# Reordering the first block of a Fourier mixing and squared-ReLU kernel: front before weight rounding, and one rounding moved into the transform

## The chip, the cores and the metric

One core of a Trainium2 chip runs the whole program. The metric is device microseconds (us) of one execution. Faster or slower means a difference of at least 2%. Engines: PE (TensorE matmul), PEld (its weight load), DVE (VectorE), ACT (ScalarE), POOL (GpSimd), SP (SyncE, which issues the loads).

## The reference, cut to what matters

```python
# x: (8, 3008, 256) float32; w_in: (256, 2048) and w_out: (2048, 256), both float64
X = np.fft.fft(np.fft.fft(x, axis=1), axis=2).real.astype(np.float32)
t = X.reshape(8 * 3008, 256)
h = t @ w_in
g = np.maximum(h, 0) ** 2
return (g @ w_out).astype(np.float32)
```

## The kernel before

The kernel folds x and makes, for each batch, three small spectra P, E and Q by products with cosine and sine tables (`dft_ops`). The transform over the 256 features is folded into w_in: for each of 8 pairs of 128-column slices of w_in, PE makes G1 and G2 ("G products", PSUM tile `pg`) and one column gE (`pe`). After that the program is a row of steps, one for each block of columns and pair j. A step has three parts:

- **front**: four products on PE into two PSUM tiles (`ph`), then `he` and two `g` for each half on DVE;
- **combine**: relu and square on ACT, then four additions on POOL (the "left sums" s1 to s4);
- **back**, two steps later: seven products on PE into four accumulators.

The weights come as float64 and are rounded to float32 on the chip (`convert`): for a pair of w_in ("win") or of w_out ("wout") a start (two DVE operations, L201 and L206, and three on ACT, L203, L204 and L208) and a finish (three DVE operations, L211, L213 and L214). A wout also needs four subtractions on POOL (the "weight sums"). Only the first block's eight steps do this; in all later steps the weights stay.

The parts that the change and the argument touch (cuts are marked):

```python
psh = ctx.enter_context(tc.tile_pool(name="psh", bufs=2, space=PSUM))   # ph and pg share it
psd = ctx.enter_context(tc.tile_pool(name="psd", bufs=2, space=PSUM))   # pd, pe, po

def load_win(j):
    w = ep.tile([P, 2, CH], F32, name="win", tag="sB" if j % 2 else "sA")
    finish = convert(w, pair_in(j))          # start now, finish later
    def then():
        finish()
        for tab, G, n in ((cosd, G1, P), (sind, G2, P - 1)):
            ps = psh.tile([P, CH], F32, name="pg", tag="h")
            ...                              # products; ACT copies to G
        ps = psd.tile([P, CH], F32, name="pe", tag="d")
        ...                                  # products; ACT copies to gE
    return then

weights = [lambda j=j: load_win(j) for j in range(2)]
for j in range(NJ):                          # NJ = 8
    if j + 2 < NJ:
        weights.append(lambda j=j: load_win(j + 2))
    weights.append(lambda j=j: load_wout(j))

def next_weight():                           # start the next, finish the one begun
    nonlocal begun
    then, begun = begun, weights.pop(0)() if weights else None
    then()
...
    # one turn of the loop over the steps
    if i < NJ:
        for _ in range(2 if i + 2 < NJ else 1):
            next_weight()                    # roundings and G products of pair i + 2
    g = front(b, k0, n, j, between)
    ...
    if i >= LAG and flight:                  # LAG = 2
        back(at[2], at[3], g_, s_, final)
    ...
    flight.append(((b, k0, n, j), g, combine(n, g)))
```

## Time and profile before

| What | Value |
|---|---|
| Time, median of 3 runs | 2051.64 us |
| Time, median of 6 runs (with the later ones) | 2051.55 us (2050.50 to 2052.09) |
| PE busy | 2004.4 of 2049.8 us |
| PE's first row, front 0 on DVE, front 8 on DVE | 11.9, 70.42, 134.35 us |
| One step of a later block on PE | 4.67 us |

The reader should take from the profile that PE does all it can from 160 us on, so the change plays entirely in the first 135 us, where DVE's roundings hold PE up. In a timeline row the bracket gives the time that the engine stood idle just before the row and what released it. The lines themselves stand in the prediction below.

### The profile page before, as it was taken

To read this page: it belongs to the slowest core of one execution; us is meant where nothing else is said; L and a number is where in the kernel's file an instruction comes from. 1 tells how busy PE (TensorE), PEld (TensorE's weight loads), DVE (VectorE), ACT (ScalarE), POOL (GpSimd) and SP (SyncE) were. 2 spreads that over 40 slices of the span, in tenths; PEclk is the share of its full clock that TensorE was granted. 3 is DMA by queue.
4 is the path that set the end of the run, shared out by engine and by line. 5 is a ranking of instruction groups with operands and counts; after the bars stand their busy time and mean duration, and the time that the engine had idled before them with its cause. 6 is when DMAs were issued, how large, how long until landed. Compare 5 with 4: busy or idle time off the path is not lost.

```text
span 2049.8 us, 27083 instructions
## 1 busy us (share of the span) xinstructions
PE 2004.4 (98%) x9464; PEld 1743.8 (85%) x9464; DVE 1337.7 (65%) x3275; ACT 952.2 (46%) x1067; POOL 1203.9 (59%) x1763
## 2 busy tenths in 40 slices
PE   6799999999999999999999999999999999999998
PEld 4588888888888888888888888888888888888887
DVE  6798666776567755777557775677656776555554
ACT  1564444544444444445444544454444444445443
POOL 0376555665556655666557665666655675556654
PEclk9899999999999999999999999999999999999999
DMA  6223000110011000011001110011001100000000
GB/s 178 88 57 59 29 11 32 41 36 21 11 41 41 26 26 30 26 31 46 11 26 36 38 29 11 31 41 36 21 11 41 41 11 16 31 11 11 21 11 20
DMA packets 66104, 68.45 MB, mean 33 GB/s; under 512 B 26297, under 2 KB 56969, under 8 KB 65968
## 3 DMA queue, kind: packets, MB, share of 16 engines
q1 hardware_dynamic: 64892, 66.21, 11.3%
q8 instruction: 74, 1.21, 0.3%
q10 hardware_dynamic: 1076, 0.52, 0.1%
q14 instruction: 62, 0.51, 0.1%
HBM read 42.03 MB, written 24.68 MB: 33 GB/s over the span
## 4 chain that ended last, share of the span: by engine, by line
PE 95%; DVE 3%; DMA 1%; issue 0%; SPq 0%; ACT 0%; DVEq 0%
PE ph L405 16%; PE mA L448 16%; PE ph L406 16%; PE mC L448 16%; PE mB L448 16%; PE mD L448 8%; PE pd L345 5%; PE po L490 2%; PE pg L229 1%; DMA xt<-in_x_dram 1%; DVE he L408 0%; DVE g L411 0%; PE pe L235 0%; DVE g L410 0%; DMA raw<-in_moe_w_in_dram 0%
## 5 line engine op out<-in xcount | busy, mean ns | idle before, releaser
L419 ACT ACTIVATE g<-g 128x1004 f32<-128x1004 f32 (+1 forms) x384 | 399.4, 1040 | 739.3 <-DVE g L411 481.9
L408 DVE SCALAR_TENSOR_TENSOR he<-Et,gE,ph 128x251 f32<-128x251 f32 (+1 forms) x768 | 362.1, 472 | 578.2 <-PE ph L406 577.7
L425 POOL TENSOR_TENSOR s<-g 128x251 f32<-128x251 f32 (+1 forms) x384 | 252.2, 657 | 671.2 <-ACT g L420 650.6
L405 PE MATMUL ph<-Pt,G 128*128 128x251 f32 (+1 forms) x1536 | 452.4, 375 | 0.5 <-DVE g L411 0.4
L406 PE MATMUL ph<-Qt,G 127*128 127x251 f32 (+1 forms) x1536 | 451.2, 374 | 0.0
L420 ACT ACTIVATE g<-g 128x1004 f32<-128x1004 f32 (+1 forms) x384 | 399.3, 1040 | 12.1
L448 PE MATMUL mA<-g,wout 128*128 128x251 f32 (+1 forms) x1536 | 389.6, 375 | 0.0
L448 PE MATMUL mC<-s,wsum 128*128 128x251 f32 (+1 forms) x1536 | 389.5, 374 | 0.0
L410 DVE TENSOR_TENSOR g<-he,ph 128x251 f32<-128x251 f32 (+1 forms) x768 | 320.6, 417 | 58.9 <-DVE he L408 0.5
L405 PEld LDWEIGHTS ph<-Pt,G 128*128 128x128 f32 x1536 | 287.8, 189 | 42.0 <-issue 3.2
L406 PEld LDWEIGHTS ph<-Qt,G 127*128 127x128 f32 x1536 | 291.2, 190 | 35.8
L448 PEld LDWEIGHTS mC<-s,wsum 128*128 128x128 f32 x1536 | 291.6, 190 | 35.3
L411 DVE TENSOR_TENSOR g<-he,ph 128x251 f32<-128x251 f32 (+1 forms) x768 | 314.2, 409 | 0.0
L448 PEld LDWEIGHTS mA<-g,wout 128*128 128x128 f32 x1536 | 281.5, 189 | 37.3 <-issue 4.0
L426 POOL TENSOR_TENSOR s<-s,g 128x251 f32<-128x251 f32 (+1 forms) x384 | 289.3, 753 | 30.1
L427 POOL TENSOR_TENSOR s<-g 128x251 f32<-128x251 f32 (+1 forms) x384 | 290.7, 757 | 0.0
L428 POOL TENSOR_TENSOR s<-g,s 128x251 f32<-128x251 f32 (+1 forms) x384 | 263.6, 686 | 0.0
L448 PE MATMUL mB<-g,wsum 128*128 128x251 f32 (+1 forms) x768 | 225.1, 374 | 0.0
L448 PE MATMUL mD<-s,wout 128*128 128x251 f32 (+1 forms) x768 | 225.0, 374 | 0.0
L448 PE MATMUL mB<-s,wout 128*128 128x251 f32 (+1 forms) x768 | 224.6, 374 | 0.0
L448 PEld LDWEIGHTS mB<-g,wsum 128*128 128x128 f32 x768 | 145.7, 190 | 17.7
L448 PEld LDWEIGHTS mD<-s,wout 128*128 128x128 f32 x768 | 144.9, 189 | 18.1
(77 smaller groups left out, 1334.1 us busy)
## 6 DMA issues: line engine op xcount, KB each, us to landing
xt<-in_x_dram SPq DMA_DIRECT2D x24, 512.0 KB
out_dram<-os SPq DMA_DIRECT2D x94, 125.0 KB
out_dram<-os SPq DMA_DIRECT2D x80, 126.0 KB
xt<-in_x_dram SPq DMA_DIRECT2D x16, 384.0 KB
Et<-e_dram SPq DMA_DIRECT2D x7, 752.5 KB
raw<-in_moe_w_in_dram SPq DMA_DIRECT2D x16, 256.0 KB
raw<-in_moe_w_out_dram SPq DMA_DIRECT2D x16, 256.0 KB
xt<-in_x_dram SPq DMA_DIRECT2D x8, 480.0 KB
```

Of the source, the lines that this page charges most:

```text
L405: nc.tensor.matmul(hP, G1[:, fs], pt[:, ks], start=True, stop=True)
L406: nc.tensor.matmul(hQ, G2[:, fs], qt[:, ks], start=True, stop=True)
L408: nc.vector.scalar_tensor_tensor(out=t, in0=et[:, ks], scalar=gE[:, fc:fc + 1], in1=hP, op0=ALU.mult, op1=ALU.add)
L410: tt(out=g[:, h, 0, 0:n], in0=t, in1=hQ, op=ALU.add)
L411: tt(out=g[:, h, 1, 0:n][:, ::-1], in0=t, in1=hQ, op=ALU.subtract)
L419: act(v, v, AF.Relu)
L420: act(v, v, AF.Square)
L425: gt(out=s1, in0=g21, in1=g22, op=ALU.add)
L426: gt(out=s2, in0=s1, in1=g11, op=ALU.subtract)
L427: gt(out=s3, in0=g11, in1=g21, op=ALU.subtract)
L428: gt(out=s4, in0=g12, in1=s2, op=ALU.subtract)
L448: nc.tensor.matmul(acc[nm][:, i, 0:n], w, v[:, 0:n], start=j == 0 and i == 0, stop=j == NJ - 1, skip_group_check=True)
```

## The change: its intent, and the diff

The intent is to start the steps earlier and to take the roundings out of the way of each step's products. In the prologue, the rounding of pair 1 moves into the gaps that DVE has while PE makes Q, and Q's joins come after both of its odd products. In a step, the front comes first, then relu, square and left sums, then the G products of the *next* pair (rounded a step ago), then the roundings: wout of this pair, win two pairs ahead.

```diff
-        return then
+        return finish, products          # load_win: G products are a part of their own
@@ weights
     for j in range(NJ):
+        weights.append(lambda j=j: load_wout(j))
         if j + 2 < NJ:
             weights.append(lambda j=j: load_win(j + 2))
-        weights.append(lambda j=j: load_wout(j))
@@ groups of the transform: odd products and their join are two entries now
-            return [(0.5, even_n), (0.5, join_4), (0.7, join_2), (1.2, odd_n)]
+            return [(0.5, even_n), (0.5, join_4), (0.7, join_2), (0.0, odd_n), (1.2, join_1)]
@@ prologue (the P and E groups are reordered in the same way; cut)
+    groups_at(20, 25)                    # Q: both even groups
     begun = weights.pop(0)()             # start of win 1
-    groups_at(16, 20, 17, 18, 19, 21, 22, 23)
-    next_weight()
+    groups_at(21, 22, 23)                # Q: joins and odd products of the first
+    products = next_weight()             # finish of win 1
+    groups_at(26, 27, 28, 24, 29)        # second's joins and odd products, then both last joins
+    products = [products]
@@ the step
-            if i < NJ:
-                for _ in range(2 if i + 2 < NJ else 1):
-                    next_weight()
             g = front(b, k0, n, j, between)
+            if i < NJ:
+                s = combine(n, g)
+            for f in products:
+                f()
+            products = [next_weight() for _ in range(2 if i + 2 < NJ else 1 if i < NJ else 0)]
```

More of the change, by code (lines that the diff above doesn't have):

```diff
@@ L222, in load_win, with products @@
         finish = convert(w, pair_in(j))
-        def then():
-            finish()
+        def products():
             for tab, G, n in ((cosd, G1, P), (sind, G2, P - 1)):
@@ L253, in then @@
             gt(out=t4, in0=t2, in1=b21, op=ALU.subtract)
-        return then
+        return then, lambda: None
     folded = {}
@@ L374, in odd_n, with join_1 @@
             def odd_n():
-                ps = psd.tile([P, 512], F32, name="pd", tag="d")[0:n, 0:n0]
-                product(ps, 3)
+                st["odd"] = psd.tile([P, 512], F32, name="pd", tag="d")[0:n, 0:n0]
+                product(st["odd"], 3)
+            def join_1():
                 dst = e_rows if b is None else PQE[b][which]
                 nh = S // 8
-                both(dst[:, kp:kp + 2 * n0 - 1:2], dst[:, M - kp - 2 * (nh - 1):M - kp + 1:2], st["c"], ps)
-            return [(0.5, even_n), (0.5, join_4), (0.7, join_2), (1.2, odd_n)]
+                both(dst[:, kp:kp + 2 * n0 - 1:2], dst[:, M - kp - 2 * (nh - 1):M - kp + 1:2], st["c"],
+                     st["odd"])
+            return [(0.5, even_n), (0.5, join_4), (0.7, join_2), (0.0, odd_n), (1.2, join_1)]
         ops = [] if b is None else [(0.0, start)]
@@ L504 @@
     for j in range(NJ):
+        weights.append(lambda j=j: load_wout(j))
         if j + 2 < NJ:
             weights.append(lambda j=j: load_win(j + 2))
-        weights.append(lambda j=j: load_wout(j))
     def next_weight():
         nonlocal begun
-        then, begun = begun, weights.pop(0)() if weights else None
-        then()
+        (finish, products), begun = begun, weights.pop(0)() if weights else None
+        finish()
+        return products
     pieces = [[f for _, f in fold(0, t)] for t in range(NT)]
@@ L536 @@
     for_p(0)
-    begun()
+    finish, products = begun
+    finish()
+    products()
     for t in range(1, 4):
         for_p(t)
-    groups_at(0, 4)
+    groups_at(0, 5)
     for_p(4)
@@ L543 @@
     for_p(5)
-    groups_at(5, 6)
+    groups_at(6, 7)
     for_p(6)
+    groups_at(3)
     for n, t in enumerate((4, 5, 6, 0, 1, 2, 3)):
         for_q(t)
-        groups_at(*((3, 7), (8,), (9, 10), (11, 12), (13, 14), (15,), ())[n])
+        groups_at(*((4, 8, 9), (10,), (11, 12), (13, 14, 15), (16, 17), (18,), (19,))[n])
+    groups_at(20, 25)
     begun = weights.pop(0)()
-    groups_at(16, 20, 17, 18, 19, 21, 22, 23)
-    next_weight()
+    groups_at(21, 22, 23)
+    products = next_weight()
+    groups_at(26, 27, 28, 24, 29)
+    products = [products]
     LAG = 2
@@ L595 @@
         if i < len(steps):
-            flight.append(((b, k0, n, j), g, combine(n, g)))
+            flight.append(((b, k0, n, j), g, s if i < NJ else combine(n, g)))
 _INS = ['x', 'moe_w_in', 'moe_w_out', 'cos_s', 'sin_s', 'cos_d', 'sin_d', 'alt_d']
```

## The prediction

> **What bounds the kernel now.** I read the page's busy shares and slices first, then the windows view over stretches that I chose from the slices, then the timelines of PE, DVE, ACT and POOL from 36 to 135 us.
>
> From the page and from the windows view (columns: stretch, its length, busy us of PE, PEld, DVE, ACT, POOL with instruction counts, granted PE clock, DMA share, GB/s):
>
> ```profile
> PE 2004.4 (98%) x9464; PEld 1743.8 (85%) x9464; DVE 1337.7 (65%) x3275; ACT 952.2 (46%) x1067; POOL 1203.9 (59%) x1763
> ...
> PE   6799999999999999999999999999999999999998
> ...
> DVE  6798666776567755777557775677656776555554
> ...
> PEclk9899999999999999999999999999999999999999
> ...
> 11.91:69.30 57.39, 45.77 (x133) 30.42 (x133) 40.88 (x111) 9.66 (x23) 0.86 (x2) 0.82 0.47 129
> 69.30:119.20 49.90, 36.85 (x165) 30.80 (x164) 44.96 (x79) 33.79 (x55) 25.42 (x39) 0.90 0.30 94
> 119.20:160.00 40.80, 40.42 (x195) 35.66 (x195) 35.88 (x80) 22.87 (x27) 30.45 (x46) 1.00 0.41 63
> 160.00:2030.00 1870.00, 1869.92 (x8925) 1637.10 (x8924) 1206.21 (x2983) 878.93 (x954) 1140.53 (x1664) 1.00 0.09 27
> ```
>
> PE is the bound: from 160 to 2030 us it is busy 1869.92 of 1870. Nothing in the change shortens that stretch, whose code stays as it is. All that it can win lies between 11.9 us, where PE starts, and 119.2 us, after which PE hardly waits. There PE stands idle 11.6 us up to 69.3 us (transform, first weights) and 13.1 us from there to 119.2 us (steps 0 to 5 of the first block), and its clock is granted at 0.82 and 0.90, so some products take double time. Even all of the idle time, 24.7 us, is 1.2% of 2051.6.
>
> What holds PE there is the loop of DVE and PE (columns: start, length, engine, line, op, out<-in, count, idle before and its releaser):
>
> ```profile
> 65.50 0.72 ACT L204 ACTIVATE fd<-fd,ramp 128x512 uint32<-128x512 f32 x1
> ...
> 66.25 0.69 DVE L211 SCALAR_TENSOR_TENSOR fd<-raw,fd 128x512 uint32<-128x512 uint32 x1 [3.42 <-ACT fd L204]
> ...
> 70.42 0.47 DVE L408 SCALAR_TENSOR_TENSOR he<-Et,gE,ph 128x251 f32<-128x251 f32 x1 [2.15 <-PE ph L406]
> ...
> 73.42 0.68 DVE L211 SCALAR_TENSOR_TENSOR fd<-raw,fd 128x512 uint32<-128x512 uint32 x1
> ...
> 76.99 1.20 DVE L211 SCALAR_TENSOR_TENSOR fd<-raw,fd 128x512 uint32<-128x512 uint32 x1
> ...
> 80.94 0.48 DVE L408 SCALAR_TENSOR_TENSOR he<-Et,gE,ph 128x251 f32<-128x251 f32 x1 [0.99 <-PE ph L406]
> ...
> 75.49 1.86 PE L229 MATMUL pg<-win,cosd 128*128 128x256 f32 x4 [4.26 <-DVE win L214]
> ...
> 116.56 1.13 PE L229 MATMUL pg<-win,cosd 128*128 128x256 f32 x4 [1.35 <-DVE win L214]
> ...
> 76.00 0.79 POOL L426 TENSOR_TENSOR s<-s,g 128x251 f32<-128x251 f32 x1
> ```
>
> The reader is to see three things. PE waits at each step for the rounding of the next pair (win L214), 4.26 us at worst. DVE waits little inside steps (0.99 us), so it is nearly the bound of these steps: 44.96 us busy of 49.9. And the first step's DVE work starts at 70.42 only, though Q, its last input, was ready at 56.7 us: DVE idles 3.42 and 2.15 us there, because ACT's share of the rounding (L203, L204) queues behind ACT copies that wait for PE.
>
> **What the Trainium skill says.**
> - "TensorE: Matmul & The Clock Gate", section "What's actually happening": after an idle window of about 3.4 us PE's clock is halved, and it takes a busy window to get it back. The trace agrees: the pg products (first of eight to last) take 3.57 us after the gap of 4.26 us and 1.99 us after one of 1.35 us.
> - The same page, "Architectural detail": ACT, DVE and GpSimd queues are strict FIFO. So program order decides; the wait of 3.42 us is of this kind.
> - "SBUF — State Buffer", "Who interferes with whom": a DVE instruction with two SBUF inputs contends with a GpSimd instruction that reads SBUF; one with at most one does not. The trace agrees: L211 takes 0.68 us with POOL idle and 1.20 at 76.99 beside POOL's left sums (the row at 76.00 is one of them); the front's DVE work (one input in PSUM) keeps its 0.42 and 0.47 us beside POOL's weight sums at 80 to 82 us.
> - "Perfetto Trace Analysis", "GPSIMD Engine Instruction": POOL spans are to be timed from start to start. I do so.
>
> **The change part by part.** Costs, all from the DVE, ACT and PE timelines, start to start. A front on DVE (he, g, g twice): 70.42 to 72.75 = 2.33 us. A rounding (L201, L206, L211, L213, L214): 72.75 to 75.43 = 2.68 us alone; beside the left sums 75.47 to 79.88 = 4.41, so 1.73 us more. Relu and square on ACT: POOL starts 2.3 us after the front. PE at full clock: front 1.70, back 2.97, one pair's G products 2.65 (116.56 to 119.20).
>
> (a) Removed from ahead of the first front: products of pairs 1 and 2 on PE (59.37 to 69.4) and the roundings of win 2 and wout 0. Pair 1's rounding moves into DVE's gaps while PE makes Q: those are 1.88, 3.82 and 1.28 us now (idle times in DVE's timeline, 45 to 56 us). ACT's copies for Q now go ahead of that pair's ACT work. I work Q out anew: last odd E join to 44.9; Q's second even group on PE to 48; ACT done with L204 at 48.2; win 1 rounded at 50.3; second joins to 51.3; the odd products, back to back, to 54 or (slow clock) 55.3; join 1 of the second to 55 or 56.3; first ph to +0.5. So the first front starts on DVE at about 56.2 instead of 70.42: 14.2 us earlier.
>
> (b) Given back: before, 14 roundings (win 1 to 7, wout 0 to 6) lie ahead of front 6 and front 6 starts at 125.95. After, wout 6 moves behind it: one rounding less, but the two of step 0 now stand between front 0 and front 1. So between front 0 and front 6 lie 12 roundings after, 10 before: 2 x 2.68 us plus contention come back.
>
> (c) Period of a step after: DVE front 2.33, two roundings 5.36, together 7.69. The left sums run on POOL from 4.6 us into the step and the weight sums now follow them, so both meet roundings: before, the weight sums met the front, which doesn't contend. I take 1.2 us for the left sums (less than 1.73, as DVE will pause in them) and 0.5 for the weight sums (as at 128.5 to 130.8 us, where L211, L213 and L214 lost about 0.5). And a new pause: ACT's order in a step is relu, square, two G copies and the gE copy, then L203, L204 of the next win. gE waits for PE, whose products now wait for the front's PSUM buffers (cos at +1.2, sin at +2.4 us); gE at 4.2 to 5.8, L204 1.5 us later at 6 to 7.3, DVE wants it at 6.6: a pause of some 0.5. Sum 9.9 us, against 10.5, 10.5, 9.5, 10.5, 9.5 of before. Steps 0 and 1 have no back, PE idles long and runs at half clock (pg 3.6), so 10.6 each.
>
> (d) PE at the end of it: front 6 on DVE at 56.2 + 2 x 10.6 + 4 x 9.9 = 117.0. PE then does pair 7's products (from +1.2, first buffer free) 2.65, back 4 2.97, front 7 1.70, back 5 2.97, and reaches front 8 at 128.5 without another wait: steps 6 and 7 have one rounding each, under PE's 4.67 us and its lead. Before, front 8 starts on PE at 133.30. Everything after is the same program. Gain 4.8 us: 2051.64 - 4.8 = 2046.8 us.
>
> (e) Splitting the join from the odd products in P and E moves PE work ahead of DVE work where DVE is 95% busy (30 to 40 us: 9.49 of 10). Worth nothing before Q, about 0.9 us for Q (its last fold ends at 44.0), counted in (a).
>
> **The rivals.**
> 1. DVE-bound, all given back. If both POOL groups cost their full contention (1.73 + 1) and ACT's pause is 1 us, the period is about 11 and front 6 starts at 122: gain about 0, 2051 us. For it: POOL's work per step and DVE's together fill the period; against it: the two can't both hold, a paused DVE contends with nothing.
> 2. PE-bound steps. If DVE slips under 9.3 us because weight sums fall beside the front again and the clock stays full (gaps under 2 us, as at 116.56), front 6 comes at 112 to 113: gain 9, 2042.5 us. For it: step 91.44 to 100.91, 9.47 us with DVE never idle; new rounding order puts five DVE operations ahead of POOL's start.
> 3. PE serial chain: the new wait of G products on the front's PSUM buffers plus slow clock (3.6 pg, 1.1 pe, 2.97 back, 1.7 front from +1.2) gives 10.6 us in every step: front 6 at 119.8, gain 2, 2049.6 us. Against it: PE's gap then shrinks under 1 us and the clock returns.
> A slower kernel needs more than all 14.2 us given back; only 1 and 3 together reach that.
>
> **Range and chances.** The prediction is 2046.8 us. Rivals 2 and 1 set the ends: 2042.8 to 2050.4 should hold it 8 times in 10. Faster by over 2% needs 41 us, more than PE's idle time and most of the clock loss: 0.005. Slower by over 2%: nothing that large is touched: 0.005. Within 2%: 0.99.
>
> **What would show it.** (a) first he of L408 near 56, Q's two odd groups back to back, win 1 rounded before Qt's first join. (b, c) distance from front to front 9.5 to 10.5 us, a wait of DVE L211 on ACT L204, weight sums stretched from 0.53 start to start, PE waiting on DVE g L411 or L410 instead of win L214. (d) first regular PE row (front 8) near 128.5, then a busy PE as before; the windows after it unchanged. Wrong would be: fronts starting late (DMA of a raw tile, which has three roundings of lead), a period under 9.3 or over 10.8, or new PE waits after step 8, where POOL now finishes the weight sums later in the step.

## The result, and the profile after

The changed kernel took 2052.46 us (median of 6, 2048.01 to 2053.41) beside 2051.55 us of the kernel before (6 runs). The ratio of their times is 1.0002, with a 95% interval of 0.9989 to 1.0015. Ratios here are the mean time of one kernel's fast runs over that of the other's in the same rounds, so they are not quite the ratio of the medians quoted. The predicted gain of 4.8 us did not come, and the median lies above the predicted range (2042.8 to 2050.4).

The windows of the changed kernel, same stretches and columns as in the prediction:

```profile
11.91:69.30 57.39, 45.03 (x132) 28.05 (x132) 45.59 (x119) 12.63 (x26) 4.44 (x5) 0.88 0.47 132
69.30:119.20 49.90, 42.09 (x160) 33.83 (x161) 44.83 (x80) 31.16 (x53) 29.49 (x40) 0.80 0.31 95
119.20:160.00 40.80, 39.58 (x189) 34.23 (x188) 32.28 (x71) 19.76 (x26) 26.54 (x40) 0.99 0.38 60
160.00:2030.00 1870.00, 1869.93 (x8925) 1637.12 (x8924) 1205.73 (x2984) 878.38 (x955) 1139.01 (x1664) 1.00 0.09 27
```

The last row is that of before (1869.93 against 1869.92): the long part of the program is untouched, as foreseen. In the second row PE is busier than before, 42.09 us against 36.85, with fewer matmuls recorded (160 against 165) at a lower clock, 0.80 against 0.90. A recorded matmul took 263 ns in the mean, against 223 (the mix of shapes is not quite the same). So PE was not given more work there, as far as the records show; it worked more slowly.

The changed kernel's timeline of DVE and PE (its L410 is L408 of the kernel before, and L228, L450, L407 and L408 are the G products, back and front on PE):

```profile
60.12 0.48 DVE L410 SCALAR_TENSOR_TENSOR he<-Et,gE,ph 128x251 f32<-128x251 f32 x1 [0.32 <-PE ph L408]
...
91.42 0.47 DVE L410 SCALAR_TENSOR_TENSOR he<-Et,gE,ph 128x251 f32<-128x251 f32 x1 [1.59 <-PE ph L408]
...
122.44 0.47 DVE L410 SCALAR_TENSOR_TENSOR he<-Et,gE,ph 128x251 f32<-128x251 f32 x1 [1.60 <-PE ph L408]
...
71.05 1.13 PE L228 MATMUL pg<-win,cosd 128*128 128x256 f32 x4 [4.09 <-DVE g L413]
...
81.04 1.13 PE L228 MATMUL pg<-win,cosd 128*128 128x256 f32 x4 [1.80 <-DVE g L413]
82.20 1.74 PE L228 MATMUL pg<-win,sind 128*127 128x256 f32 x4
...
85.29 2.02 PE L450 MATMUL mA<-g,wout 128*128 128x251 f32 x4
...
102.39 1.13 PE L228 MATMUL pg<-win,cosd 128*128 128x256 f32 x4 [1.82 <-DVE g L413]
```

Front 0 does come earlier, at 60.12 instead of 70.42. But the G products now wait for `g` on DVE, because they share the two PSUM buffers of `psh` with the front; before, they waited for the rounding. Behind such a gap (4.09 us, 1.80 us) the clock falls: the first G products still take 1.13 us, the next 1.74, and the four products of mA take 2.02 us, where a full clock needs 1.01. Now the *back* stands behind the G products, ahead of the next front, so the half clock lands on it, and DVE waits 1.59 us for the next front. The gap of 1.82 us at 102.39 had no such effect. In the slow steps DVE also waits for ACT L204 (0.91 us in step 1, 0.66 in step 2, 0.95 in step 5), and in no others.

The same steps as windows, from one `he` of a front's first half to the next:

```profile
60.12:69.75 9.63, 5.82 (x28) 4.22 (x26) 9.46 (x16) 6.49 (x11) 4.83 (x6) 1.00 0.17 54
69.75:79.74 9.99, 8.16 (x24) 6.13 (x24) 8.91 (x17) 6.57 (x11) 6.43 (x10) 0.66 0.35 106
79.74:91.42 11.68, 10.36 (x35) 8.65 (x36) 9.25 (x18) 6.59 (x12) 6.84 (x10) 0.71 0.37 113
91.42:101.03 9.61, 8.63 (x42) 6.79 (x40) 9.44 (x16) 6.50 (x11) 4.82 (x6) 1.00 0.28 83
101.03:110.69 9.66, 7.83 (x38) 6.41 (x38) 9.42 (x17) 6.49 (x11) 6.05 (x9) 1.00 0.35 109
110.69:122.44 11.75, 10.35 (x35) 8.62 (x36) 8.96 (x18) 6.59 (x11) 7.21 (x11) 0.71 0.24 73
```

The first number after the comma is PE's busy time, the third DVE's; the clock is the last but two. Four steps take 9.6 to 10.0 us and two take 11.7; both of the long ones have a clock of 0.71. Step 1 has 0.66, but no back stands in it yet, and it takes only 9.99 us.

So the theory to test was: **the clock** takes the gain back, through a gap on PE that the new order makes. The rivals were: **DVE's contention with POOL** (the weight sums now meet roundings), **ACT's order** (DVE waits for L204), and simply **late loads** in the profiled execution: its first cosT join on DVE starts at 24.28 us against 22.41.

### The profile page after: what moved, and what is told of

The parts are those of the page before. It is cut to its first block, busy times and chain, and to the rows that moved or that the text cites. A ratio compares the mean times of both kernels' runs of the same rounds, so it can differ in the third digit from the quotient of the medians.

```text
span 2051.2 us, 27084 instructions
## 1 busy us (share of the span) xinstructions
PE 2009.5 (98%) x9464; PEld 1744.3 (85%) x9464; DVE 1337.1 (65%) x3275; ACT 950.3 (46%) x1067; POOL 1206.1 (59%) x1763
## 4 chain that ended last, share of the span: by engine, by line
PE 94%; DVE 4%; DMA 1%; issue 0%; ACT 0%; SPq 0%; DVEq 0%; ACTq 0%
PE mA L450 16%; PE mC L450 16%; PE mB L450 16%; PE ph L407 16%; PE ph L408 16%; PE mD L450 8%; PE pd L344 5%; PE po L492 2%; DMA xt<-in_x_dram 1%; PE pg L228 1%; DVE he L410 0%; DVE fd L211 0%; DVE fs L213 0%; DVE g L412 0%; DVE g L413 0%; DMA raw<-in_moe_w_in_dram 0%
## 5 line engine op out<-in xcount | busy, mean ns | idle before, releaser
L410 DVE SCALAR_TENSOR_TENSOR he<-Et,gE,ph 128x251 f32<-128x251 f32 (+1 forms) x768 | 362.1, 471 | 580.6 <-PE ph L408 580.0
L407 PE MATMUL ph<-Pt,G 128*128 128x251 f32 (+1 forms) x1536 | 453.1, 376 | 1.2 <-DVE g L413 0.6
L408 PE MATMUL ph<-Qt,G 127*128 127x251 f32 (+1 forms) x1536 | 452.2, 375 | 0.2 <-DVE Qt L357 0.2
L450 PE MATMUL mA<-g,wout 128*128 128x251 f32 (+1 forms) x1536 | 391.9, 377 | 0.0
L450 PE MATMUL mC<-s,wsum 128*128 128x251 f32 (+1 forms) x1536 | 389.8, 375 | 0.0
L407 PEld LDWEIGHTS ph<-Pt,G 128*128 128x128 f32 x1536 | 288.9, 189 | 43.6 <-issue 3.7
L408 PEld LDWEIGHTS ph<-Qt,G 127*128 127x128 f32 x1536 | 291.7, 190 | 36.6 <-DVE Qt L357 0.6
L450 PEld LDWEIGHTS mC<-s,wsum 128*128 128x128 f32 x1536 | 292.1, 190 | 35.6
L450 PEld LDWEIGHTS mA<-g,wout 128*128 128x128 f32 x1536 | 282.2, 190 | 37.3 <-issue 4.0
L450 PE MATMUL mB<-g,wsum 128*128 128x251 f32 (+1 forms) x768 | 226.0, 375 | 0.0
L450 PE MATMUL mB<-s,wout 128*128 128x251 f32 (+1 forms) x768 | 225.5, 375 | 0.0
L450 PE MATMUL mD<-s,wout 128*128 128x251 f32 (+1 forms) x768 | 225.0, 374 | 0.0
L450 PEld LDWEIGHTS mB<-g,wsum 128*128 128x128 f32 x768 | 146.2, 190 | 17.9
L450 PEld LDWEIGHTS mB<-s,wout 128*128 128x128 f32 x768 | 145.1, 189 | 18.0
```

Source lines behind the costliest of these rows:

```text
L407: nc.tensor.matmul(hP, G1[:, fs], pt[:, ks], start=True, stop=True)
L408: nc.tensor.matmul(hQ, G2[:, fs], qt[:, ks], start=True, stop=True)
L410: nc.vector.scalar_tensor_tensor(out=t, in0=et[:, ks], scalar=gE[:, fc:fc + 1], in1=hP, op0=ALU.mult, op1=ALU.add)
L450: nc.tensor.matmul(acc[nm][:, i, 0:n], w, v[:, 0:n], start=j == 0 and i == 0, stop=j == NJ - 1, skip_group_check=True)
```

## The experiments

All kernels are correct unless it is said. The table works out three times from each trace's DVE timeline: the start of front 0, the six steps from there to front 6, and the time from the start of the last Q join to front 8, which leaves out how late the loads came.

| Kernel | Median us (range) | Ratio to before (95%) | Front 0 | Six steps | Last Q join to front 8 |
|---|---|---|---|---|---|
| before (first three runs) | 2051.64 (2051.47 to 2052.09) | | 70.42 | 55.5 | 78.6 |
| changed | 2052.46 (2048.01 to 2053.41) | 1.0002 (0.9989 to 1.0015) | 60.12 | 62.3 | 76.7 |
| e1 changed again | 2051.73 (2048.52 to 2053.27) | 0.9999 (0.9985 to 1.0013) | 58.40 | 62.3 | 76.7 |
| e2 PE kept busy | 2046.09 (2045.32 to 2046.62) | 0.9972 (0.9960 to 0.9985) | 57.63 | 57.8 | 72.2 |
| e3 back first, win's ACT work first | 2045.22 (2044.38 to 2046.62) | 0.9969 (0.9956 to 0.9982) | 57.23 | 57.7 | 71.8 |
| e4 no weight sums (wrong result) | 2048.04 (2047.55 to 2048.96) | 0.9983 (0.9968 to 0.9997) | 56.37 | 57.7 | 75.4 |
| e5 before, PE kept busy | 2049.61 (2046.76 to 2054.21) | 0.9994 (0.9982 to 1.0006) | 71.13 | 52.7 | 76.8 |
| e6 first half, new rounding order | 2088.27 (2085.15 to 2090.27) | 1.0180 (1.0167 to 1.0193) | 67.47 | 91.0 | 113.0 |
| e7 second half alone | 2051.77 (2051.53 to 2054.82) | 1.0008 (0.9996 to 1.0020) | 59.46 | 63.2 | 79.9 |
| e8 PE kept busy, wout a step later | 2048.79 (2046.85 to 2049.63) | 0.9987 (0.9974 to 1.0000) | 58.02 | 54.4 | 73.2 |
| e9 first half alone | 2046.22 (2043.97 to 2050.84) | 0.9981 (0.9968 to 0.9995) | 65.08 | 55.5 | 73.1 |
| e10 back first | 2043.61 (2042.15 to 2045.33) | 0.9966 (0.9954 to 0.9979) | 55.73 | 58.2 | 70.4 |
| e11 e3 with idle products in the prologue | 2046.53 (2044.26 to 2047.86) | 0.9978 (0.9966 to 0.9991) | 56.90 | 57.7 | 74.8 |
| e12 three gaps filled | 2047.02 (2045.32 to 2051.10) | 0.9987 (0.9974 to 0.9999) | 57.05 | 57.8 | 72.2 |

As a check that nothing else matters: front 8 of the profiled run of e10 starts 9.51 us before that of the kernel before (124.84 against 134.35), and its span is 9.4 us shorter (2040.4 against 2049.8). For the changed kernel these are 1.18 and 1.4 us later and longer. In all traces but one the two differences agree within 0.3 us, so they arise before front 8; in e8 another 1.8 us are lost after it.

### e1: the changed kernel again

No edit.

> The changed kernel once more, for a second trace and more times. Theory clock: the two steps of the first trace that took 11.7 us from front to front (the others took 9.6 to 10.0) are those in which PE's clock fell to half in its gap of about 1.8 us; [...]here one to three steps of 11 to 12 us, at other places, and times spread over 3 us or more. Theory order (rival): the long steps come from the program itself and are the same two, steps 2 and 5. Theory start (rival for part of the loss): the first DVE row came 0.75 us later and the first cosT join 1.9 us later than in the kernel before because its loads came late; here they come as in the kernel before (within 0.5 us). Median 2050 to 2052.5 us in all of them.

Measured: the same two steps were long, 2 and 5, with 11.68 and 11.75 us, though the loads came as in the kernel before (first cosT join at 22.57) and everything stood 1.7 us earlier. So the expectation that the long steps would be at other places failed; in these two traces they are tied to the program. Late loads explain a part of front 0 in the first trace, and nothing of the steps. The time was again that of the kernel before.

### e2: PE kept busy in its gaps

```diff
             g = front(b, k0, n, j, between)
+            if i < NJ:
+                keep = psd.tile([P, CH], F32, name="keep", tag="d")     # nobody reads it
+                for _ in range((0, 8, 8, 3, 3, 3, 3, 0)[i]):
+                    nc.tensor.matmul(keep[:, 0:n], G1[:, j * P:(j + 1) * P],
+                                     PQE[b][0][:, k0:k0 + n], start=True, stop=True)
```

> Changed kernel plus idle products on PE (0, 8, 8, 3, 3, 3, 3 of 0.42 us) between a step's front and the G products of the next pair, into a PSUM tile that nobody reads: PE's gaps in steps 1 to 6 shrink under 1.2 us. Theory clock: the clock stays at 1.0 there, no step over 10.3 us, DVE waits for PE less than 0.5 us a step, front 6 about 58.5 us after front 0 (62.3 in the first trace), 3 to 4 us faster than the changed kernel. Theory DVE (rival): the steps are DVE's own time, so that the period stays at 9.6 to 10 in the short steps and the sum falls by under 1.5 us. Theory harm: the idle products delay the G products and the kernel is slower by 1 us or more.

Measured, as windows from front to front:

```profile
76.84:86.45 9.61, 8.90 (x44) 7.37 (x44) 9.44 (x18) 6.53 (x11) 6.13 (x9) 1.00 0.35 111
...
105.74:115.42 9.68, 9.10 (x45) 7.54 (x44) 9.44 (x18) 6.50 (x11) 6.07 (x9) 1.00 0.20 57
```

These are steps 2 and 5, the long ones of the changed kernel. The clock is 1.00, DVE is busy 9.44 of 9.61 us and waits for nothing; all six steps take 9.60 to 9.68. Useless work on PE makes the program 5.6 us faster than e1, which ran on the same chip: the clock theory holds, and the gain is more than the 3 to 4 us expected. It is a clean test of the steps, as the idle products feed nobody and every other instruction is the same. Of the 5.3 us by which front 8 comes earlier than in e1's trace, 4.5 lie in the six steps; the other 0.8 is an earlier front 0, ahead of every idle product, and not their doing. DVE's waits for ACT L204 are gone too, so they came with the slow clock: the rival of ACT's order falls with it. The runs spread over 1.3 us instead of 5.

### e3 and e10: back ahead of the G products

e10 changes only the order on PE:

```diff
             if i < NJ:
                 s = combine(n, g)
+                if i >= LAG:
+                    at, g_, s_ = flight.pop(0)
+                    back(at[2], at[3], g_, s_, False)
             for f in products:
                 f()
...
-        if i >= LAG and flight:
+        if i >= NJ and flight:
```

e3 has that edit and one more, the start of the next win (and with it ACT's L203, L204 and L208) ahead of the G products:

```diff
+            ahead_of = [next_weight()] if i < NJ else []
             for f in products:
                 f()
-            products = [next_weight() for _ in range(2 if i + 2 < NJ else 1 if i < NJ else 0)]
+            products = ahead_of + [next_weight() for _ in range(1 if i + 2 < NJ else 0)]
```

> Changed kernel with the order on PE front, back, G products (it was front, G products, back) for the first eight steps, and the next win's ACT work ahead of the copies of G. Back fills the time in which the G products wait for the front's PSUM buffers. Theory clock and PSUM wait: PE waits under 1 us a step from step 2 on, no step over 10.2 us from step 2, DVE doesn't wait for ACT L204, front 6 about 58 us after front 0, 3 to 5 us faster than the changed kernel. Theory DVE: period stays 9.6 to 10, gain under 1.5 us. Harm: the later G copies hold up the next front, DVE waits for PE over 1 us a step, no gain.

> Only one of the two edits of the fast version: back ahead of the G products on PE, ACT's order as in the changed kernel (G copies, then the win's ACT work). Back fills PE's gap of 1.8 us, so the clock theory wants no long steps of 11.7; but gE then comes last on PE at about 6.5 us into the step, ACT's share of the win rounding starts after it, and DVE waits for ACT L204 about 1.5 us a step: periods 10 to 11, total 2047 to 2050. If it equals the version with both edits (2045.2), ACT's order doesn't matter; if it is as slow as the changed kernel (2051.7), the gap on PE wasn't the cause.

(The "fast version" here and in e11 is e3.)

e3's steps all took 9.58 to 9.67 us, and DVE never waited for ACT L204, as its clock theory said. But PE's waits did not fall under 1 us, and the clock did not stay at 1.00. A row of e3's PE timeline, and two of its steps as windows:

```profile
112.16 0.69 PE L407 MATMUL ph<-Pt,G 128*128 128x251 f32 x2 [2.20 <-ACT G L229]
...
76.42:86.01 9.59, 9.59 (x44) 8.36 (x43) 9.42 (x18) 6.59 (x11) 6.11 (x9) 0.86 0.35 112
...
105.25:114.92 9.67, 7.47 (x36) 6.55 (x35) 9.43 (x18) 6.47 (x11) 6.06 (x9) 0.92 0.16 55
```

PE's wait only moved: the next front now waits for ACT's copies of G, and spells of half clock follow. They cost these steps nothing, because PE stands ahead of DVE there: front 6 is on PE at 112.16, and DVE reaches it at 114.92 without a wait. So here the clock cost time only where slow products stood on the path, and not wherever it fell.

For e10 I expected periods of 10 to 11, because gE would come late and DVE would wait for ACT. That was wrong: e10 is as fast as e3, and DVE waited for ACT L204 once, 0.95 us. Its PE timeline shows why (a stretch of one step; rows of back after mA are left out):

```profile
80.19 0.68 PE L407 MATMUL ph<-Pt,G 128*128 128x251 f32 x2
...
81.99 1.01 PE L450 MATMUL mA<-g,wout 128*128 128x251 f32 x4
...
86.22 1.13 PE L228 MATMUL pg<-win,cosd 128*128 128x256 f32 x4 [1.09 <-DVE g L413]
```

PE runs ahead of DVE: front 3 is on PE at 80.19, while DVE reaches it at 84.92. The back fits into that lead, and so delays nothing: the G products start 1.3 us after the front's first DVE row, as in the changed kernel. PE's gap is 1.09 instead of 1.8 us, and from step 2 on the clock is 1.00 in every step. Also, between front 6 and front 7 stand no longer the G products *and* the back with their waits (6.21 us instead of 8.49; in e3 it was still 8.13, as its front 6 came late on PE and its back behind that). ACT's order, the second edit of e3, is not needed. e3 and e10 can't be told apart by time; e10 is the one to keep, as the smaller edit: 2043.61 us beside 2050.31 us of the kernel before in the same rounds, ratio 0.9966.

### e4: without the weight sums

```diff
-            gt(out=t3, in0=b22, in1=b12, op=ALU.subtract)        # and the three after it
+    nc.gpsimd.memset(wsum.rearrange("p a j h -> p (a j h)"), 0.5)   # once, ahead of everything
```

The result is wrong.

> Changed kernel without the four POOL weight sums of each pair (their tile is filled once with a constant: wrong result on purpose). They now follow the left sums and meet the win rounding on DVE. Theory contention: L214 of win falls from 0.83 to 0.69 and L213 by about 0.1, together 0.2 to 0.5 us a step, so the short steps go from 9.6 to 9.2 or 9.4, and the six steps lose 1.5 to 3 us. Theory clock: long steps stay, sum of six steps falls by under 1.5 us. Time within 2 us of the changed kernel in either case.

The last rounding of win on DVE beside the weight sums (changed kernel), and without them (e4, where it is L215):

```profile
88.99 0.83 DVE L214 SCALAR_TENSOR_TENSOR win<-fs,fd 128x512 f32<-128x512 f32 x1
```

```profile
94.30 0.69 DVE L215 SCALAR_TENSOR_TENSOR win<-fs,fd 128x512 f32<-128x512 f32 x1
```

The contention is real and small: the short steps take 9.45 to 9.56 us instead of 9.60 to 9.69, less than the 0.2 to 0.4 us expected. The kernel was nevertheless 3.7 us faster than e1, more than the 2 us that I had allowed. In the traces front 8 comes 3.4 us earlier. Of this, 2.0 us lie ahead of front 0, where no weight sum has run (the last Q join waited 1.40 us for PE instead of 3.37). The six steps gave 4.7 us, as steps 2 and 5 stayed short, and the step after front 6 took 3.3 us of that back, as it became long (11.82 us instead of 8.49) at a clock of 0.71. So most of the difference is again the clock, whose spells fell on other steps in this trace.

### e5: the kernel before, PE kept busy

```diff
         if i < len(steps):
+            if i < NJ:
+                ...                     # as in e2, with (8, 8, 3, 3, 3, 3, 0, 0)
             flight.append(((b, k0, n, j), g, combine(n, g)))
```

> The kernel before (old order) plus idle products on PE (8, 8, 3, 3, 3, 3 of 0.42 us) at the end of steps 0 to 5, in PE's wait for the next pair's rounding. Does the clock cost the old order as much as the new one? Theory clock of the new order: in the old order the half clock falls on the G products (3.6 instead of 2.0 us), of which at most 1 us a step is on the path (DVE waited 0.96 to 0.99 us for PE in three of six steps): gain at most 3 us, probably 1.5 to 2.5. If it gains 4 us or more, the two orders are equal when both are warm, and the change itself is worth nothing.

Its six steps took 52.7 us against 55.5, so 2.8 us went: DVE's three waits for PE (0.99, 0.96, 0.97). The time gained 1.9 us in the median, but its interval holds 1, so the trace is the better evidence here. The old order loses less to the clock, because in it the half clock falls on the G products, and only a part of that is on the path.

### e6, e9 and e7: the two halves apart

e6 and e9 keep the new prologue and put the roundings and G products ahead of the front again:

```diff
+            if i < NJ:
+                for f in products:
+                    f()
+                products = []
+                for _ in range(2 if i + 2 < NJ else 1):
+                    next_weight()()
             g = front(b, k0, n, j, between)
```

e6 forgot to restore the old order of roundings (win, then wout); e9 does.

> Only the first half of the change: pair 1's rounding in Q's gaps and the joins after the odd products; the steps in the old order (roundings and G products ahead of the front). The first front on DVE then comes after pair 1's products, two roundings and pair 2's products: it comes 3 to 7 us earlier than in the kernel before (70.4), at 64 to 67, and the steps have the old periods (9.5 to 10.5), so front 8 on PE comes at 128 to 131 (133.3 before) and the kernel is 2 to 4.5 us faster than before, faster than the whole change. If instead it is within 1 us of the kernel before, the rounding of pair 1 wasn't on the path either.

> The first half of the change alone, this time with the old order of roundings too (win before wout in each step; the first try kept wout before win, so that DVE rounded the next win last and then waited for its G products, 7.25 us a step). First front on DVE at 62 to 67 (70.4 before), then periods of 9.5 to 10.5 as in the kernel before; front 8 on PE at 127 to 131; 2 to 4.5 us faster than the kernel before. If it reaches 2047 to 2049, the gain is the earlier rounding of pair 1 and the new step order takes it back through the clock; if it is within 1 us of the kernel before, the first half is worth nothing.

e6 failed as a test of the prologue, though it teaches something. DVE rounds wout, then win, and then has to wait for that win's G products before its own next front; from its DVE and PE timelines:

```profile
84.39 0.48 DVE L410 SCALAR_TENSOR_TENSOR he<-Et,gE,ph 128x251 f32<-128x251 f32 x1 [7.25 <-PE ph L408]
```

```profile
77.19 2.07 PE L228 MATMUL pg<-win,cosd 128*128 128x256 f32 x4 [8.91 <-DVE win L214]
```

PE waits 8.91 us for DVE and DVE 7.25 us for PE in the same step: nothing overlaps, and 37 us are lost. The new order of roundings is only good with the new place of the front.

e9 is the clean test: front 0 at 65.08 us (expected 62 to 67), then periods that are those of the kernel before (10.53, 10.47, 9.46, 10.51, 9.53, 5.00). It was faster than the kernel before by 0.05 to 0.32%, about 4 us (1.0 to 6.6). So **the first half of the change brings a gain by itself, by its mean nearly all of the predicted one**. With the second half on top, the time from Q's last join to front 8 grows from 73.1 to 76.7 us.

e7 has the new steps with the old order of the prologue:

```diff
-    groups_at(20, 25)
     begun = weights.pop(0)()
-    groups_at(21, 22, 23)
-    products = next_weight()
-    groups_at(26, 27, 28, 24, 29)
+    groups_at(20, 25, 21, 22, 23, 24, 26, 27, 28, 29)
+    products = next_weight()
@@ the P and E groups are put back in the same way; cut
```

> Only the second half: the new step, with the old prologue order (joins with their odd products, pair 1's rounding after Q). Q ends later (its second odd products wait for the first's join): first front 1 to 2 us later than with the whole change, then the same steps of 9.6 and 11.7 us. 0 to 2.5 us slower than the whole change.

Measured: steps 2 and 5 long again (12.60 us, behind a gap of 4.06 us on PE, and 11.74, behind one of 1.82), and the time of the kernel before. Front 0 did not come 1 to 2 us later: at 59.46 us it lies between the two traces of the whole change.

### e8: each wout rounding a step later

```diff
     for j in range(NJ):
-        weights.append(lambda j=j: load_wout(j))
+        if j:
+            weights.append(lambda j=j: load_wout(j - 1))
         if j + 2 < NJ:
             weights.append(lambda j=j: load_win(j + 2))
+    weights.append(lambda: load_wout(NJ - 1))
```

with the idle products of e2 and (1, 2, 2, 2, 2, 2, 1, 2) roundings a step.

> Changed kernel with idle products (0, 2, 8, 3, 3, 3, 3) and each wout rounding one step later, so that 11 roundings instead of 12 stand between front 0 and front 6. If DVE is the bound of warm steps, that takes one rounding with its contention (2.7 to 4 us) out of the path: first period 6 to 7 us instead of 9.6, the others 9.6, 2 to 4 us faster than the changed kernel with idle products alone (2046.1): 2042 to 2044. If PE or ACT takes over, or the weight sums come too late for the back, the gain is under 1 us.

The first part came: step 0 took 6.10 us, and the six steps 54.4 us. But it was lost again at the end, where two roundings fall into step 7:

```profile
132.24 1.21 PE L450 MATMUL mB<-g,wsum 128*128 128x251 f32 x2 [5.09 <-POOL wsum L252]
```

The back has to wait 5.09 us for the weight sums of a wout that was rounded too late. So the 2042 to 2044 us expected did not come (2048.79): the work was moved, not removed.

### e11 and e12: where the clock falls

e11 is e3 with five idle products on PE between the groups of E and Q; e12 is e2 with idle products only after fronts 1, 2 and 5, (0, 8, 8, 0, 0, 3, 0, 0).

> The fast version (back first, the win's ACT work first) plus five idle products on PE between the E and Q groups, against the half clock there, in which the wait of the last Q join for PE is 1.40 us in some traces and 3.37 in others. If the clock is held: that wait at 1.4 or less, first front at 55.5 to 57, total 2043.5 to 2045. If the idle products only delay Q (PE is DVE-bound there): 2045 to 2047.

> Dose of the idle products: only in the gaps ahead of the two slow spells of the changed kernel's traces (8 after front 1, 8 after front 2, 3 after front 5); the gaps of 1.8 us after fronts 3, 4 and 6 stay. Clock theory: the long steps 2 and 5 become 9.6 to 9.9, front 6 at 57.8 to 58.8 after front 0, total 2046 to 2047. If other steps become long instead (a slow spell moves to another gap of 1.8 us), 60 us or more from front 0 to front 6, total 2047.5 to 2050: then any gap of 1.8 us may drop the clock.

e11 gained nothing on e3. The wait of the last Q join for PE was 1.41 us, but that was so in e3 too, so this run can't tell whether the idle products did it. After front 6 a gap of 2.21 us on PE (the next front waits for ACT's copies of G) brought a spell of half clock, and this step took 9.06 us instead of 8.13, the next 6.66 instead of 4.60.

In the trace of e12 the gaps that were left open are these:

```profile
87.15 1.13 PE L228 MATMUL pg<-win,cosd 128*128 128x256 f32 x4 [1.74 <-DVE g L413]
96.82 1.13 PE L228 MATMUL pg<-win,cosd 128*128 128x256 f32 x4 [1.82 <-DVE g L413]
...
116.17 1.13 PE L228 MATMUL pg<-win,cosd 128*128 128x256 f32 x4 [1.82 <-DVE g L413]
```

None of them cost the clock, and the six steps took 57.8 us. Filling three gaps was enough in this execution. But two of its five runs took 2050.2 and 2051.1 us, without a trace of them; they may have had such a spell. What decides between a gap of 1.8 us that drops the clock and one that doesn't stays open.

## Why the prediction was wrong

**The bound** was read rightly: PE's long stretch did not move, and all differences arise before front 8.

**Step (a), front 0 at about 56.2 us**, was 3.9 us too early for the profiled run (60.12) and 2.2 us for the second trace (58.40). In the profiled run the late loads account for 1.7 us (its first cosT join came 1.71 us after that of the second trace). The mis-sized term common to both traces is Q's second odd products: in both, the last Q join waited 3.37 us for them, at half clock. I had allowed 1.3 us for this, as an alternative, and taken the middle. In ten traces with the new prologue (without idle products in it) this wait was 3.0 to 3.4 us in four and 1.4 in six; in three with the old prologue it was 1.3 each time. In the four of the six that have the new steps, front 0 came at 55.7 to 57.6 us, so this step held where the clock did. Why only the new one is hit is not settled.

**Step (b)** was right in kind and miscounted. Twelve roundings do lie between front 0 and front 6 (rows of L214 in the trace), but before there were 11, and not 10 (3 of the 14 lie ahead of front 0): one is given back, not two. The slip did not reach the predicted time, which step (c) builds from the costs of a step. How much comes back shows beside e9, which keeps win 2 and wout 0 ahead of front 0: counted from the last Q join, e2 starts front 0 7.8 us earlier and reaches front 8 only 0.9 us earlier. It gives back 2.3 us in the six steps and 4.7 us between front 6 and front 8.

**Step (c), 9.9 us a step with 10.6 for the first two**, is the step that failed in kind. DVE's own period is 9.6 us (e2): front 2.33, two roundings 5.36, contention 1.9, no pause for ACT. I had taken 1.7 and 0.5 for the last two, so this part is right within 0.3 us. What failed is the sentence against rival 3: "PE's gap then shrinks under 1 us and the clock returns". That holds only right after a long step (gaps of 0.49 us at 92.72 and 0.57 at 123.81); a step at full clock opens the gap of 1.8 us again. The mean clock was 0.71 in steps 2 and 5, which took 11.7 us. My sum of the six steps, 60.8 us, is near the measured 62.3 only because I had put slow steps where there were none: steps 0 and 1 took 9.6 and 10.0 us. At full clock the sum is 57.8, so the clock costs 4.5 us there, about the whole gain that was predicted. I had seen half clocks on the G products, but never asked which instructions would stand behind the new gap: the back, on the path to the next front. And I took gaps under 2 us as harmless (rival 2), though the trace of the kernel before had this row:

```profile
105.97 1.63 PE L229 MATMUL pg<-win,cosd 128*128 128x256 f32 x4 [1.90 <-DVE win L214]
```

Behind that gap of 1.90 us four G products took 1.63 us and the next four 1.91, against 1.13 and 1.03 behind the gap of 1.35 us.

**Step (d), 11.5 us from front 6 on DVE to front 8 on PE**, was 12.04: the G products wait for the PSUM buffers in turn, so 4.3 us pass until the back starts, where I had 1.2 + 2.65. The sum of the three errors in the first trace, 3.9 + 1.5 + 0.5 = 5.9 us, brings the predicted 128.5 to the measured 134.48 within 0.1 us.

**The rivals.** Rival 1 (a period of about 11 us from contention and ACT's pause) falls: at full clock the period is 9.6 us with all of the contention in it (e2), and the weight sums are 0.15 us of that (e4). Rival 3 was the right one in two steps of six, for the reason that it names, the new wait on PSUM buffers with a slow clock; but it kept the back at 2.97 us, which took 5.08 us in step 2 (85.29 to 90.37). Rival 2 was not reached: DVE needs 9.6 us a step in this order, with no wait at all. The clearest lesson is the direction of the two halves: the first gains about 4 us alone (e9), the second gives it back through the clock (e2, e3, e10), and with back ahead of the G products the gain stays (e10; in its trace front 8 comes 2.7 us sooner after Q than in e9, though the intervals of the two times overlap).

## What to carry to other kernels

When an order of instructions on PE is changed, list PE's new gaps and, for each, what runs right behind it: if that is on the path to the next wait, a drop of the clock can double its time (mA: 2.02 us instead of 1.01). Work that only has to be done some time, here the back of two steps ago, belongs into the gap where PE would wait for a buffer, not behind it; a few idle products into a spare PSUM tile are a quick test of whether the clock is the cause. And test the halves of a change one by one: here one half had the gain, and the other hid it.

## What the Trainium skill lacked or had wrong

- "TensorE: Matmul & The Clock Gate", section "What's actually happening": the halved clock is tied to an idle window of about 3.4 us. Here it also fell behind gaps of 1.80 us (changed kernel, at 81.04 and 112.06) and 1.90 us (kernel before, at 105.97), and did not behind gaps of 1.82 us (at 102.39), of 1.74 and 1.82 us (e12) and of 2.22 us (e11, at 111.86). The page's section "A second HAM failure mode: psum-queue depth-cycling" has it that frequent short idle times can make the clock swing; it gives no length for them.
- The same section calls the window free-running and the onset variable from run to run. In both traces of the changed kernel the same two steps (2 and 5) were slow, though the second trace stood 1.7 us earlier; in e4, where the gaps of the short steps were 1.31 to 1.70 us, it was the step after front 6. Two traces are too few to call the page wrong here.
- "SBUF — State Buffer", "Who interferes with whom": it says which operations contend, but not what a mixed stream costs. The traces agree for the operations with two SBUF inputs. L201 and L206, which read one, also grew beside the left sums, from 0.42 us to 0.74 and 0.94 (kernel before, at 75.47 and 76.13); the page keeps such operations free of contention only outside certain modes of DVE, and no trace shows the mode. Here four left sums and the weight sums on POOL added 1.9 us to the five DVE operations of one rounding (4.58 instead of 2.68 us).
- No page gives the price of letting G products and front share a PSUM pool: here a wait for a rounding was traded against one for a buffer, of 1.8 us in the short steps with a back.
